# Top-32 attention and a leaky-ReLU MLP on one core: one reciprocal for two units, the even unit's split moved, weight pieces spread differently

## The chip, the cores and the metric

The kernel runs on one core of one Trainium2 chip. A core has a matrix engine (TensorE, "PE" in the profile; its weight loads are listed apart as "PEld"), a vector engine (VectorE, "DVE"), a scalar engine (ScalarE, "ACT"), a general engine (GpSimd, "POOL") and a queue engine (SyncE, "SP") that issues most of the DMAs. Each engine runs its own instructions in order and waits on semaphores for the others.

The metric is the device time of one execution in microseconds. Before the change it is 1431.69 us, the median of three runs (1431.59 to 1433.73). One further execution was profiled: 1433.87 us, of which the profile's span is 1431.8 us.

## What is computed

```python
# q, k, v: (8 batches, 8 heads, 576 tokens, 64)
scores = scale * q @ k.T                       # scale = 1/8
kth    = the 32nd largest score of each row
scores = where(scores >= kth, scores, -1e9)
attn   = exp(scores - rowmax)
attn   = attn / (attn.sum(-1) + 1e-9)
x      = attn @ v, heads side by side          # (4608 tokens, 512)
h      = x @ w_in                              # (4608, 2048)
out    = maximum(0.01 * h, h) @ w_out          # (4608, 512)
```

Everything is float32. The weights come in as 64-bit floating point numbers and are put together on the chip.

## The kernel before, in words

**Units.** Two heads of one batch make a pair of heads; 128 query rows of such a pair (both heads, so 2 x 576 scores per partition) make a *unit*. There are 144 units. Batch by batch, 16 units have whole blocks of 128 rows, and two gather the 64 rows left over of two pairs of heads each. `steps` is the list of the units, and the kernel goes through them two at a time: an *even* step s and an *odd* step s+1 make one turn of the main loop. The text calls units s and s+1 a pair of units.

**What happens to a unit.** PE computes the scores (L237), ACT copies them to `s_sb` (L246). DVE finds the 32 largest (`top_k`, L263): it folds the 576 scores into a maximum and a minimum half (two TENSOR_TENSOR on L270, one for each head), and then alternates MAX8 (L276) and MATCH_REPLACE8 (L281) four times. `limits` (L285) makes two small vectors, on ACT (`nleast`) and on POOL (`nbias`, L292 and L293). `mask` (L295) and `exponents` (L299) run on ACT and leave the row sums in `z`; `sums` (L303) adds 1e-9 on ACT and writes `ze`; `reciprocals` (L307) is one DVE instruction on a 128x2 tile; `normalize` (L311) multiplies, one ACT instruction for each head. `split` (L314) then takes the float32 weights apart into two 16-bit halves, two POOL copies of 128x1152 with a DMA to DRAM behind each, and `transpose` (L324) reads them back transposed by a DMA transpose into `wT` (three buffers). With `wT`, PE weighs the values (`weigh_whole`, L356, L365 in the profile), and the result is copied by ACT into `x` (L388).

**Order of the work.** The order is written out by hand, engine by engine, in `even` (L729) and `odd` (L781). In step s the unit itself (`cur`) is searched; the unit before it (`old`) gets its limits, mask and exponents; the one before that (`older`) is finished. So an even unit s has its exponents and `sums` in odd step s+1, and its reciprocal, normalization, split and transpose at the start of even step s+2. An odd unit s+1 has its exponents, `sums`, reciprocal and normalization within even step s+2, and its split and transpose in odd step s+3. Both are weighed at the end of even step s+4 (`values_at`, L637). The generator `picks` lets the DVE search be cut: in the even step the old unit's reciprocal stands after the third round, so one pair of MAX8 of this unit and then the odd unit's L270 follow.

**The MLP.** When all units of 128 tokens (the first four chunks, `EARLY`) or of 256 tokens are weighed, a chunk of the MLP becomes ready (`attended`). Its matmuls are fed to PE in slices: `mlp_steps(budget)` is called seven times in each step, and each call emits matmuls up to a budget. Evictions of a finished PSUM tile (ACT, L492 for `gT`, L526 for `o_sb`) are put off to the next `catch_up`. The large chunks use a seven-product scheme, whose sums of matrices (`gT`, `top`, `o_sb` on L443) run on POOL: `sum_now(2)` late in the even step, `sum_now(3)` in the odd step.

**The first four units.** `first_steps` (L839) handles units 0 to 3 and at the same time rounds the weights: 16 pieces (the first in two parts), each read by a DMA of 1 MB, copied on POOL (L129), worked on by ACT, PE and DVE (L135 to L158). `round_more` moves the queue of pieces on by one. Before the change it is called twice in each of units 0 and 1, three times in each of units 2 and 3, and the rest after them, where DVE has no search to do. `BESIDE` decides from which piece on the even ones use the `narrow` PSUM tile.

Of the kernel before, what the change touches and what calls it, by code (L numbers as in the profile page):

```python
# [20 lines left out]
def kernel(  # L21
# [13 lines left out]
    nc = tc.nc  # L35
# [64 lines left out]
    FIRST = 4  # L100
    BESIDE = 2 * FIRST + 3

# [182 lines left out]
    def limits(u):  # L285

        largest, least_kept = u.tops[:, :, 0, 0], u.tops[:, :, ROUNDS - 1, 7]
        u.nleast = small.tile([P, 2], F32, name="nleast")
        u.nbias = small.tile([P, 2], F32, name="nbias")
        u.z = small.tile([P, 2], F32, name="z")  # L290
        nc.scalar.activation(u.nleast, least_kept, AF.Copy, bias=0.0, scale=-1.0)  # L291
        nc.gpsimd.tensor_tensor(u.nbias, least_kept, largest, ALU.subtract)  # L292
        nc.gpsimd.tensor_scalar(u.nbias, u.nbias, SCALE, None, ALU.mult)  # L293
# [8 lines left out]

    def sums(u):  # L303
        u.ze = small.tile([P, 2], F32, name="ze")
        nc.scalar.activation(u.ze, u.z, AF.Copy, bias=1e-9, scale=1.0)

    def reciprocals(u):  # L307
        u.rz = small.tile([P, 2], F32, name="rz")
        nc.vector.reciprocal(u.rz, u.ze)  # L309

# [326 lines left out]
    def values_at(n):  # L637

        return (n | 1) + (2 if n in HASTY else 3)

    steps = units

    def unit(n):
# [3 lines left out]
    for n, u in enumerate(steps):  # L647
        ch, _ = x_at(u.b * S + u.q0)
        done_tokens[ch] += u.rows * len(u.pairs)
        if done_tokens[ch] == CHUNKS[ch] * HP:  # L650
            ready_at.append(((values_at(n) | 1) if n >= FIRST else FIRST - 1, ch))
    assert [ch for _, ch in ready_at] == list(range(len(CHUNKS)))
# [20 lines left out]
    with tc.manual_schedule():  # L673
# [41 lines left out]
        def values(s, spare):  # L715
            weighed = []
            for n in range(FIRST, len(steps), 2):
                if values_at(n) != s:
# [10 lines left out]
        def even(s):  # L729
# [5 lines left out]
            next(picks, None)  # L735
            if older:
                reciprocals(older)
            for _ in range(4):
# [7 lines left out]
            catch_up()  # L746
            if older:
                normalize(older, 0)
                normalize(older, 1)
                if not in_haste:  # L750
                    split(older)
                    transpose(older)
                else:
                    transpose_in_haste(older)
            mlp_steps(budget)
            if old:
                exponents(old, 0)
                exponents(old, 1)
                sums(old)
            if older and in_haste:  # L760
# [20 lines left out]
        def odd(s, new, ps, weighed):  # L781
# [12 lines left out]
            if older and not in_haste:  # L794
                split(older)
                transpose(older)
            keep(weighed)
            if new:
                keep_scores_of(new, ps)
            if older and in_haste:  # L800
                transpose_in_haste(older)
                if old:
                    exponents(old, 0)
                    exponents(old, 1)
                    sums(old)
                keep_transposed(older)
# [11 lines left out]
            if old and not in_haste:  # L818
                exponents(old, 1)
                sums(old)  # L820
            for _ in range(4):
# [17 lines left out]
        def first_steps():  # L839

            load_weights(0)
            load_qk(0)
            load_weights(1)
# [3 lines left out]
            load_qk(3)  # L847
            next(jobs[0], None)
            round_more()
            first = first_scores(steps[0])  # L850
            next(first, None)
            next(first, None)
            round_more()
            first = first_scores(steps[1])
            next(first, None)
            new = ps = None
            for s in range(FIRST):
# [6 lines left out]
                next(picks, None)  # L864
                if s < 2:
                    next(picks, None)
                if s == 0:
# [7 lines left out]
                if old:  # L875
                    exponents(old, 0)
                    exponents(old, 1)
                    sums(old)
                if s < 2:
                    next(picks, None)  # L880
                next(picks, None)
                next(picks, None)
                round_more()
                if old:
                    reciprocals(old)
                    normalize(old, 0)
                    normalize(old, 1)
                if s >= 2:
                    next(picks, None)
                    next(picks, None)  # L890
                    round_more()
                for _ in picks:
# [17 lines left out]
            exponents(b, 1)  # L910
            sums(b)
            round_more()
            reciprocals(b)
# [5 lines left out]
            round_more()  # L919
# [75 lines left out]
```

## Time and profile before

| | |
|---|---|
| median of three runs | 1431.69 us |
| profiled execution | 1433.87 us |
| its span | 1431.8 us |
| DVE busy | 1319.2 us (92%) |
| PE busy | 1347.2 us (94%) |
| ACT busy | 1023.0 us (71%) |
| POOL busy | 709.8 us (50%) |
| DVE MAX8, L276 | 636.3 us, 1152 instructions |
| DVE MATCH_REPLACE8, L281 | 460.6 us, 864 instructions |
| DVE TENSOR_TENSOR, L270 | 212.8 us, 288 instructions, mean 778 ns |
| DVE RECIPROCAL, L309 | 21.7 us, 144 instructions, mean 151 ns |
| POOL COPY, L321 (split) | 316.8 us, 284 instructions, mean 1144 ns |

How to read it: a line of the profile names the source line, the engine, the operation, what it writes and reads, and the shapes. "Busy" is the union of the spans of a group. In a timeline each line begins with the start in us and the time from the first start to the last end of the group; `x2` means two instructions put together, and a bracket gives the idle time of the engine before it and what ended it. A matmul's end is modelled, so that PE's busy share says less than it seems to. The chain of work that ended last is followed back from the last instruction, at each step to what released it.

### The profile page before, as it was taken

Reading aid. Unit: us, or ns where it says so; the run is one execution under the profiler, and the core shown is the slowest. Engines: PE = TensorE matmul, PEld = TensorE weight load, DVE = VectorE, ACT = ScalarE, POOL = GpSimd, SP = SyncE. Lnnn points to the kernel's source line nnn. Section 1 sums busy time; section 2 is a strip of 40 time slices with the busy share of each in tenths; the row PEclk is TensorE's granted clock in tenths of the full one; section 3 lists DMA queues with packets and bytes.
Section 4 is the critical chain, followed back from the end, with each engine's and each line's share of the span. In section 5 each row is a group of like instructions: output and inputs, shape, how many; then the busy total and the mean of one; then the engine's idle time right before and its main releaser. Section 6 shows DMA issues by size and latency. Waiting matters only on the chain.

```text
span 1431.8 us, 27705 instructions
## 1 busy us (share of the span) xinstructions
PE 1347.2 (94%) x9794; PEld 1031.4 (72%) x9794; DVE 1319.2 (92%) x3412; ACT 1023.0 (71%) x2144; POOL 709.8 (50%) x796
## 2 busy tenths in 40 slices
PE   6679599969999999999999999999999999999998
PEld 2234354447778888878888888888878888888887
DVE  7989999899999999999999999999999999999700
ACT  6866767677777777777777777777777777777621
POOL 2332373335555555555555555555555555555512
PEclk9889899989999999999999999999999999999999
DMA  7772545655666556756666556655676565655400
GB/s 291 250 222 67 140 134 172 193 141 133 165 185 174 144 144 186 196 152 139 177 175 173 141 164 174 186 142 155 175 182 168 141 157 142 169 145 136 125 12 15
DMA packets 399388, 224.91 MB, mean 157 GB/s; under 512 B 339216, under 2 KB 348432, under 8 KB 397328
## 3 DMA queue, kind: packets, MB, share of 16 engines
q1 hardware_dynamic: 398096, 222.08, 56.9%
q8 instruction: 77, 1.26, 0.4%
q10 hardware_dynamic: 1152, 1.05, 0.2%
q14 instruction: 63, 0.52, 0.1%
HBM read 46.14 MB, written 93.19 MB: 97 GB/s over the span
## 4 chain that ended last, share of the span: by engine, by line
DVE 70%; PE 18%; issue 6%; ACT 4%; DMA 1%; POOL 0%; DVEq 0%; POOLq 0%; ACTq 0%
DVE tops L276 34%; DVE pairs L281 26%; DVE pairs L270 7%; PE ph L504 4%; PE pz L518 4%; PE ph L405 3%; PE pz L596 2%; PE wide L365 2%; DMA raw<-in_weights_dram 1%; DVE rz L309 1%; PE wide L237 1%; ACT s_sb L300 1%; ACT s_sb L312 1%; DVE w_in L158 1%; PE narrow L237 0%
## 5 line engine op out<-in xcount | busy, mean ns | idle before, releaser
L276 DVE MAX8 tops<-pairs 128x8 f32<-128x288 f32 (+1 forms) x1152 | 636.3, 592 | 0.3 <-DVE rz L309 0.3
L504 PE MATMUL ph<-x,w_in 128*128 128x256 f32 x2048 | 457.5, 382 | 4.7 <-ACT gT L492 4.4
L281 DVE MATCH_REPLACE8 pairs<-tops,pairs 128x288 f32<-128x288 f32 (+1 forms) x864 | 460.6, 539 | 0.0
L504 PEld LDWEIGHTS ph<-x,w_in 128*128 128x128 f32 x2048 | 384.3, 190 | 84.0 <-issue 16.5
L321 POOL COPY split<-s_sb 128x1152 uint16<-128x1152 uint16 x284 | 316.8, 1144 | 186.1 <-ACT s_sb L312 186.1
L312 ACT ACTIVATE s_sb<-s_sb,rz 128x576 f32<-128x576 f32 x288 | 207.1, 766 | 151.6 <-DVE rz L309 151.5
L292 POOL TENSOR_TENSOR nbias<-tops 128x2 f32<-128x2 f32 x144 | 70.2, 488 | 401.5 <-DVE tops L276 398.0
L518 PE MATMUL pz<-w_out,gT 128*128 128x256 f32 x1024 | 226.5, 379 | 0.0
L270 DVE TENSOR_TENSOR pairs<-s_sb 128x576 f32<-128x576 f32 x288 | 212.8, 778 | 12.1 <-ACT s_sb L261 2.4
L300 ACT ACTIVATE s_sb<-s_sb,nbias 128x576 f32<-128x576 f32 x288 | 223.9, 785 | 0.0
L518 PEld LDWEIGHTS pz<-w_out,gT 128*128 128x128 f32 x1024 | 194.5, 190 | 26.6 <-issue 0.2
L297 ACT ACTIVATE s_sb<-s_sb,nleast 128x576 f32<-128x576 f32 x288 | 207.6, 768 | 4.7
L365 PE MATMUL wide<-wT,vt 128*64 128x128 f32 (+1 forms) x2560 | 156.4, 284 | 27.0 <-DMA wT<-apart 26.1
L365 PEld LDWEIGHTS wide<-wT,vt 128*64 128x64 f32 (+1 forms) x2560 | 128.3, 138 | 64.4 <-issue 34.0
L518 PE MATMUL pz<-raw,top 128*128 128x256 f32 x512 | 117.3, 384 | 4.6 <-ACT o_sb L526 4.4
L518 PEld LDWEIGHTS pz<-raw,top 128*128 128x128 f32 x512 | 95.2, 190 | 28.0 <-issue 8.0
L237 PE MATMUL wide<-kt,qt 64*64 64x352 f32 x1136 | 110.2, 458 | 0.0
L246 ACT COPY s_sb<-wide 128x704 f32<-128x704 f32 x142 | 108.0, 761 | 1.7 <-PE wide L237 1.7
L492 ACT ACTIVATE gT<-ph 128x512 f32<-128x512 f32 x128 | 75.3, 588 | 29.5 <-PE ph L504 29.5
L293 POOL TENSOR_SCALAR nbias<-nbias 128x2 f32<-128x2 f32 x144 | 84.7, 588 | 12.6
L291 ACT ACTIVATE nleast<-tops 128x2 f32<-128x2 f32 x144 | 28.6, 198 | 86.4 <-DVE tops L276 85.6
L526 ACT COPY o_sb<-pz 128x256 f32<-128x256 f32 x112 | 41.8, 374 | 60.8 <-PE pz L518 60.4
(70 smaller groups left out, 1238.4 us busy)
## 6 DMA issues: line engine op xcount, KB each, us to landing
apart<-split SPq DMA_DIRECT2D x284, 288.0 KB, 2.1
raw<-in_weights_dram SPq DMA_DIRECT2D x15, 1024.0 KB, 5.3
vt<-in_vk_dram SPq DMA_DIRECT2D x32, 320.0 KB, 3.8
qt<-in_qT_dram SPq DMA_DIRECT2D x32, 288.0 KB, 3.5
kt<-in_kT_dram SPq DMA_DIRECT2D x32, 288.0 KB, 3.6
out_dram<-o_sb SPq DMA_DIRECT2D x64, 128.0 KB, 2.2
wT<-apart SPq DMA_TRANSPOSE x142, 4.6
raw<-in_weights_dram SPq DMA_DIRECT2D x2, 512.0 KB, 4.3
```

What stands on the lines that cost most here:

```text
L237: nc.tensor.matmul(to[r0:r0 + LEFT, i, :], qt[d, q0:q0 + LEFT], kt[d, k0:k1], start=True, stop=True)
L246: nc.scalar.copy(u.both[:, :, k0:k1], to)
L270: nc.vector.tensor_tensor(pairs[:, :, n, :], u.both[:, :, 0:HS], u.both[:, :, HS:S], op)
L276: nc.vector.max(out=u.tops[:, i, r, :], in_=rest[i])
L281: nc.vector.match_replace(out=rest[i], in_to_replace=u.tops[:, i, r, :], in_values=rest[i], imm_value=LOWEST)
L297: nc.scalar.activation(u.s[i], u.s[i], AF.Prelu, bias=u.nleast[:, i:i + 1], scale=1.0, alpha=BELOW)
L300: nc.scalar.activation(u.s[i], u.s[i], AF.Exp, bias=u.nbias[:, i:i + 1], scale=SCALE, accum_out=u.z[:, i:i + 1])
L312: nc.scalar.activation(u.s[i], u.s[i], AF.Copy, bias=0.0, scale=u.rz[:, i:i + 1])
L321: nc.gpsimd.tensor_copy(split, pairs[:, :, h])
L365: nc.tensor.matmul(po[n * D:(n + 1) * D, side, 0:P], v_of[u.pairs[0]][k, at, side, :], u.wT[k, at + side * NKC if at + 1 < NKC else at, :] ...
L504: nc.tensor.matmul(ph[:, i, 0:n], w_in[c][:, f * P:(f + 1) * P], x[:, c, 0:n], start=(c == 0), stop=(c == HP - 1),)
L518: nc.tensor.matmul(to, g[:, f, :], w(f), start=(first and f == 0), stop=(f == HALF - 1), skip_group_check=not first)
```

## The change

There are three parts.

1. In `even`, a pair of units (s-2, s-1) gets one `ze` and one reciprocal on a 128x4 tile (`inverses_of_pair`) instead of two of each on 128x2. `z` becomes one tile for the pair. The shared reciprocal stands where the odd unit's stood, after the third round of the search in the even step. The last two units, which are finished in haste, and the first four keep their own.
2. The even unit's normalization and split, which stood at the start of the even step, now follow the shared reciprocal, after the even step's last MAX8 and one slice of MLP. Its transpose moves to the odd step, behind the odd unit's split and directly ahead of the odd unit's transpose.
3. In `first_steps` the first scores are computed before the first weight piece (a part of `qT` and `kT` is loaded first), each of the four units has three calls of `round_more`, and the values of units 0 to 3 are weighed at the end of even step 4, so that the first MLP chunk becomes ready in step 5 instead of step 3. `BESIDE` goes from 11 to 13.

```diff
-    BESIDE = 2 * FIRST + 3
+    BESIDE = 3 * FIRST + 1
...
-        u.z = small.tile([P, 2], F32, name="z")
+        if u.first is None:
+            u.of_pair = small.tile([P, 2, 2], F32, name="z")
+            u.z = u.of_pair[:, 0, :]
+        else:
+            u.z = u.first.of_pair[:, 1, :]
...
+    def inverses_of_pair(first, second):
+        ze = small.tile([P, 2, 2], F32, name="ze")
+        nc.scalar.activation(ze, first.of_pair, AF.Copy, bias=1e-9, scale=1.0)
+
+        def reciprocals():
+            rz = small.tile([P, 2, 2], F32, name="rz")
+            nc.vector.reciprocal(rz, ze)
+            first.rz, second.rz = rz[:, 0, :], rz[:, 1, :]
+
+        return reciprocals
...
-        return (n | 1) + (2 if n in HASTY else 3)
+        return (n | 1) + (2 if n in HASTY else 3) if n >= FIRST else FIRST
...
         def even(s):
...
-            if older:
-                reciprocals(older)
+            if in_haste:
+                older.invert()
...
-            if older:
+            if in_haste:
                 normalize(older, 0)
                 normalize(older, 1)
-                if not in_haste:
-                    split(older)
-                    transpose(older)
-                else:
-                    transpose_in_haste(older)
+                transpose_in_haste(older)
             mlp_steps(budget)
             if old:
                 exponents(old, 0)
                 exponents(old, 1)
-                sums(old)
+                invert = inverses(old) if in_haste else inverses_of_pair(older, old)
...
             if old:
-                reciprocals(old)
+                invert()
             for _ in picks:
                 pass
-            for _ in range(4):
+            mlp_steps(budget)
+            if older and not in_haste:
+                normalize(older, 0)
+                normalize(older, 1)
+                split(older)
+            for _ in range(3):
                 mlp_steps(budget)
...
         def odd(s, new, ps, weighed):
...
             if older and not in_haste:
                 split(older)
+                transpose(unit(s - 3))
                 transpose(older)
...
         def first_steps():
 
+            qk_of[0] = [loads.tile([P, S], F32, name=name) for name in ("qt", "kt")]
+            nc.sync.dma_start(qk_of[0][0][:, 0:P], qT[0][:, 0:P])
+            nc.sync.dma_start(qk_of[0][1], kT[0])
             load_weights(0)
-            load_qk(0)
+            nc.sync.dma_start(qk_of[0][0][:, P:S], qT[0][:, P:S])
...
-                if s >= 2:
-                    next(picks, None)
-                    next(picks, None)
-                    round_more()
+                next(picks, None)
+                next(picks, None)
+                round_more()
...
-            weighed = weigh(steps[0:2], ps_sc.tile([P, 2, 512], F32, name="wide", bufs=2))
-            round_more()
-            transpose(b)
             while begun[0] <= len(jobs):
                 round_more()
-            weighed += weigh(steps[2:4], ps_sc.tile([P, 2, 512], F32, name="wide", bufs=2))
-            keep(weighed)
-            attended(FIRST - 1)
+            transpose(b)
             load_more(FIRST - 1)
```

More of the change, by code (lines that the diff above doesn't have):

```diff
@@ L301, in exponents, with inverses, reciprocals @@
                              accum_out=u.z[:, i:i + 1])
-    def sums(u):
+    def inverses(u):
         u.ze = small.tile([P, 2], F32, name="ze")
         nc.scalar.activation(u.ze, u.z, AF.Copy, bias=1e-9, scale=1.0)
-    def reciprocals(u):
-        u.rz = small.tile([P, 2], F32, name="rz")
-        nc.vector.reciprocal(u.rz, u.ze)
+        def reciprocals():
+            u.rz = small.tile([P, 2], F32, name="rz")
+            nc.vector.reciprocal(u.rz, u.ze)
+        return reciprocals
+    def inverses_of_pair(first, second):
+        ze = small.tile([P, 2, 2], F32, name="ze")
+        nc.scalar.activation(ze, first.of_pair, AF.Copy, bias=1e-9, scale=1.0)
+        def reciprocals():
+            rz = small.tile([P, 2, 2], F32, name="rz")
+            nc.vector.reciprocal(rz, ze)
+            first.rz, second.rz = rz[:, 0, :], rz[:, 1, :]
+        return reciprocals
     def normalize(u, i):
@@ L637, in values_at @@
     def values_at(n):
-        return (n | 1) + (2 if n in HASTY else 3)
+        return (n | 1) + (2 if n in HASTY else 3) if n >= FIRST else FIRST
     steps = units
+    for n, u in enumerate(steps):
+        u.first = steps[n - 1] if n % 2 else None
     def unit(n):
@@ L650 @@
         if done_tokens[ch] == CHUNKS[ch] * HP:
-            ready_at.append(((values_at(n) | 1) if n >= FIRST else FIRST - 1, ch))
+            ready_at.append((values_at(n) | 1, ch))
     assert [ch for _, ch in ready_at] == list(range(len(CHUNKS)))
@@ L716, in values @@
             weighed = []
-            for n in range(FIRST, len(steps), 2):
+            for n in range(0, len(steps), 2):
                 if values_at(n) != s:
@@ L758, in even @@
                 exponents(old, 1)
-                sums(old)
-            if older and in_haste:
+                invert = inverses(old) if in_haste else inverses_of_pair(older, old)
+            if in_haste:
                 keep_transposed(older)
             if old:
-                reciprocals(old)
+                invert()
             for _ in picks:
                 pass
-            for _ in range(4):
+            mlp_steps(budget)
[4 more added lines that the diff above has]
+            for _ in range(3):
                 mlp_steps(budget)
@@ L804, in odd @@
                     exponents(old, 1)
-                    sums(old)
                 keep_transposed(older)
@@ L819, in odd @@
                 exponents(old, 1)
-                sums(old)
+            if s - 1 in HASTY:
+                old.invert = inverses(old)
             for _ in range(4):
@@ L847, in first_steps @@
             load_qk(3)
-            next(jobs[0], None)
-            round_more()
             first = first_scores(steps[0])
@@ L852, in first_steps @@
             next(first, None)
+            next(jobs[0], None)
             round_more()
@@ L864, in first_steps @@
                 next(picks, None)
-                if s < 2:
-                    next(picks, None)
                 if s == 0:
@@ L877, in first_steps @@
                     exponents(old, 1)
-                    sums(old)
-                if s < 2:
-                    next(picks, None)
+                    invert = inverses(old)
                 next(picks, None)
@@ L884, in first_steps @@
                 if old:
-                    reciprocals(old)
+                    invert()
                     normalize(old, 0)
                     normalize(old, 1)
-                if s >= 2:
-                    next(picks, None)
-                    next(picks, None)
-                    round_more()
+                next(picks, None)
+                next(picks, None)
+                round_more()
                 for _ in picks:
@@ L910, in first_steps @@
             exponents(b, 1)
-            sums(b)
+            invert = inverses(b)
             round_more()
-            reciprocals(b)
+            invert()
             normalize(b, 0)
@@ L917, in first_steps @@
             split(b)
-            weighed = weigh(steps[0:2], ps_sc.tile([P, 2, 512], F32, name="wide", bufs=2))
-            round_more()
-            transpose(b)
             while begun[0] <= len(jobs):
                 round_more()
-            weighed += weigh(steps[2:4], ps_sc.tile([P, 2, 512], F32, name="wide", bufs=2))
-            keep(weighed)
-            attended(FIRST - 1)
+            transpose(b)
             load_more(FIRST - 1)
```

## The prediction

> **What bounds the kernel now.** I read the page first: busy times, then the chain that ended last.
>
> ```profile
> span 1431.8 us, 27705 instructions
> PE 1347.2 (94%) x9794; PEld 1031.4 (72%) x9794; DVE 1319.2 (92%) x3412; ACT 1023.0 (71%) x2144; POOL 709.8 (50%) x796
> ...
> DVE 70%; PE 18%; issue 6%; ACT 4%; DMA 1%; POOL 0%; DVEq 0%; POOLq 0%; ACTq 0%
> ```
>
> VectorE (DVE) carries 70% of the chain. Windows of three pairs of units each show how near the rival is (columns: stretch, length, busy us of PE, PEld, DVE, ACT, POOL, then PE's granted clock, DMA share, GB/s); the first is an early pair.
>
> ```profile
> 150.52:168.16 17.64, 7.94 (x76) 5.42 (x76) 17.50 (x47) 11.87 (x26) 6.54 (x9) 0.71 0.62 153
> 679.60:732.52 52.92, 52.52 (x398) 43.23 (x397) 52.50 (x139) 40.41 (x88) 31.05 (x34) 1.00 0.67 176
> ```
>
> DVE is full from the first pairs on, PE only later. Up to about 1260 the chain is DVE's top-32 search almost without a break, one pair per 17.64 us; after 1265 it is PE, working off MLP matmuls until the end.
>
> Then one pair in order of time: DVE, ACT, POOL.
>
> ```profile
> 713.78 1.45 DVE L270 TENSOR_TENSOR pairs<-s_sb 128x576 f32<-128x576 f32 x2
> 715.15 0.15 DVE L309 RECIPROCAL rz<-ze 128x2 f32<-128x2 f32 x1
> 721.14 0.15 DVE L309 RECIPROCAL rz<-ze 128x2 f32<-128x2 f32 x1
> 722.64 1.43 DVE L270 TENSOR_TENSOR pairs<-s_sb 128x576 f32<-128x576 f32 x2
> ```
> ```profile
> 715.34 1.44 ACT L312 ACTIVATE s_sb<-s_sb,rz 128x576 f32<-128x576 f32 x2
> 721.32 1.44 ACT L312 ACTIVATE s_sb<-s_sb,rz 128x576 f32<-128x576 f32 x2 [2.53 <-DVE rz L309]
> ```
> ```profile
> 713.76 0.20 POOL L292 TENSOR_TENSOR nbias<-tops 128x2 f32<-128x2 f32 x1 [3.85 <-DVE tops L276]
> 716.84 2.23 POOL L321 COPY split<-s_sb 128x1152 uint16<-128x1152 uint16 x2 [2.21 <-ACT s_sb L312]
> 719.04 1.28 POOL L443 TENSOR_TENSOR top<-gT 128x512 f32<-128x512 f32 x1
> 720.40 1.28 POOL L443 TENSOR_TENSOR top<-top,gT 128x512 f32<-128x512 f32 x1
> 722.68 0.77 POOL L292 TENSOR_TENSOR nbias<-tops 128x2 f32<-128x2 f32 x1 [1.01 <-DVE tops L276]
> ```
>
> See that POOL has finished its long work (split, two sums) before L270 of the odd unit at 722.64. Last, the one late place where it hasn't:
>
> ```profile
> 1342.63 2.66 DVE L270 TENSOR_TENSOR pairs<-s_sb 128x576 f32<-128x576 f32 x2
> 1341.64 1.28 POOL L443 TENSOR_TENSOR top<-gT 128x512 f32<-128x512 f32 x1
> 1343.00 1.67 POOL L443 TENSOR_TENSOR top<-top,gT 128x512 f32<-128x512 f32 x1
> ```
>
> L270 took 2.66 instead of 1.43: its second half stood still while POOL did the second sum. MAX8 and MATCH_REPLACE8 beside a split keep their 0.44 and 0.74.
>
> **The change part by part.**
>
> *Reciprocals.* 144 become 75: units 4 to 141 (69 pairs) share one, which sits where the odd unit's was. In the pair above L270 to the first MAX8 takes 715.23-713.78 = 1.45 with the reciprocal between, 723.98-722.64 = 1.34 without; the next MAX8s are 0.02 shorter after it. 69 x 0.09 = -6.2 us, on the path. Bounds from what a reciprocal holds up in these rows, 0.07 to 0.15: -4.8 to -10.4.
>
> *The even unit's normalization and split.* They move from the start of the even step to behind that shared reciprocal. From 721.14 on, every gap is rigid: normalization 0.18 after the reciprocal, split 1.50 after that (715.34 to 716.84), so 1.68 after it; odd L270 1.50 after it (722.64-721.14). The split's first half will thus arrive 0.18 us into L270's first half, in each of 69 pairs. What happens then I take from the rows: nbias at 722.68, also just behind L270's start, needs 0.20 when alone (713.76) but ends 0.81 after L270's start, so it got in at 0.61. The split half (2.23/2, say 1.14) would run from 0.61 to 1.75. In the 1342.63 case L270 ended 0.62 after POOL (1345.29 and 1344.67). So L270 ends at 2.37 instead of 1.43: 69 x 0.94 = +64.9. Lower bound 0 (POOL waits until both halves are through; nothing in it can gain). Upper: an early pair of splits delayed two DVE operations, 1.33 and 1.36 instead of 0.42, 1.85 together: +128. I keep to 0.94, because the 1342.63 row is the same instruction with POOL waiting, 0.8 to 1.1 for the range.
>
> The Trainium skill (SBUF — State Buffer, "SBUF: two separate sides") says that the two engines share one port pair, locked for a whole instruction, the loser blocked, and that DVE operations with two SBUF inputs take part. By it the price would be the whole half split, 1.14 x 69 = 79, and the sum 14 higher; it also speaks against the place chosen.
>
> *What stands behind the split on POOL.* Two sums (pitch 1.35), the odd step's nbias, the other split, then the odd step's sums of gT. From the even L270 as 0: split halves 9.4-10.5 and 11.0-12.1, two sums to 14.8, nbias to 15.6, split to 17.8, then one sum (15 pairs), three (14) or none, 1.24 each. The next even L270 starts at 17.64-0.09+0.94 = 18.5. One sum ends at 19.0 and costs 0.4; of three, the second gets between the halves: 1.46. 14 x 1.86 = +26; bounds 0 (POOL 1 us earlier for one, none between) and 14 x 3.2 = +45 (two full collisions of 1.2 to 2).
>
> nbias later by 5 us: exponentials on ACT wait for it, but have until the shared reciprocal; ze was ready 2.5 us early (the wait at 721.32) and no longer has the 1.44 of normalization ahead. Cost 0; without this cover 1 us a pair.
>
> *SP and PE.* The even split's two DMAs issue later, and both transposes follow the odd split. They land about 7 us into the next even step; PE's weighing (718.74, 5.0 into it) then waits 2 us, and scores, loads and stores behind them slip likewise. The copies of scores end 4 us before DVE needs them, and PE gains 1 us of slack a pair from the slower DVE: cost 0; beyond 4 us, DVE would pay all of it. MLP evictions now stand behind the normalization on ACT: same cover.
>
> *First four units.* Scores first: the first L270 had waited 2.4 us. By kt's 3.6 us to landing, 2 us of matmul, 1.2 of copies and the first rounding behind them, I estimate it at 11.4 instead of 11.83. Two of six weight pieces move from the bare tail into the units; the tail's DVE waits are 1.46, 0.40 and 2.69, of which I take 3.0 as gone. Together -3.4; bounds +1 (copies delay rounding) and -7.0 (all). Chunk 0's MLP starts a step later: PE idles 9.7 of 17.64 in the first window above, which takes it. The fourth transpose must wait for weighing to free one of three wT buffers, holding SP; only a load of v is behind it, and scores needed 15 us later: 0, or 4.6 without cover.
>
> *Stalls.*
>
> ```profile
> DVE rz L309 <- ACT ze L305: 16.0, 7, 8.0
> ```
>
> Of these, 5.5 lie between 120 and 290, where ACT came late behind PE, and 2.3 at 1341. With the normalization out of the way and a slower DVE they go: -7.8 (bounds 0, -7.8). The old delay at 1342.63, 1.2, is counted in the 69 and comes off. What is late next is the port.
>
> *End.* From the last MAX8 (1352.5) to the end are 79 us. PE enters less behind; ACT's 4.6 us delay before the last limits, mostly behind PE, goes: -5 (0 to -6).
>
> **Sum:** -6.2+64.9+26-3.4-7.8-1.2-5 = +67.3. The profiled execution took 1433.87 (span 1431.8 and 2.1 around it), 2.2 over the median of the three runs; 1433.9+67.3 = 1501.2, less 2.2: **1499 us**.
>
> **The rivals.**
>
> (a) *No collision:* the split slips in only after L270 (it would have to come 0.43 later, or DVE keep the port for both halves). Then -6.2-3.4-5.5 remains, PE is fuller, and transposes 2 us later show at the end: about -13, 1419 us, faster. It decides where the split arrives past 0.61 after L270's start. For it: no row shows this split beside L270. Against: POOL and DVE took turns in the split rows (81.8 and 83.0, 90.6 and 91.6) and at 1342.63. 0.13.
>
> (b) *Splits collide, sums don't:* 1473. POOL's order has to run some us ahead of my addition. 0.20.
>
> (c) *Late transposes become the bound:* landing over 4 us beyond the old weighing, each further us costs 69; 1.3 us more gives about 1590. The order of queues allows it, the slack speaks against. 0.03.
>
> (d) *Gains and collisions cancel* (collision below 0.3 us): 1432. 0.03.
>
> My forecast's mechanism has 0.61; with (b) and (c), slower has 0.84, faster 0.13, within 0.2% (what a measurement of this kernel can tell from none) 0.03. Range: 0.8 a pair and no sums give 1433+55-6-7-9-5 = 1461, 1.1 and 45 give 1543; a little is added below: 1452 to 1542.
>
> **What would show it.** Odd L270 at about 2.4 instead of 1.43, split recorded as starting inside it and stretched; every fourth even L270 near 2.9; the period 18.5 to 20; 75 reciprocals; PE's share down. Odd L270 at 1.43 beside the split would prove me wrong at once; PE waits on wT with L270 waiting for scores would mean (c).

## The result, and the profile after

The changed kernel takes **1518.22 us** (median of four runs, 1515.71 to 1518.71) against 1432.71 us of the kernel before beside it (1431.59 to 1436.97), so 85.5 us slower; the ratio on record is 1.0588 with a 95% interval of 1.0562 to 1.0613 (the two medians alone give 1.0597). The prediction was 1499 us with a range of 1452 to 1542: the sign and the main mechanism held, the forecast was 19 us short.

The profiled execution took 1518.17 us with a span of 1516.4 us, 84.6 more than before. The page of the kernel after, its busy times, its chain and three of its groups (the numbers after the bar are busy time and mean ns of one, then idle time before):

```profile
span 1516.4 us, 27555 instructions
PE 1379.0 (91%) x9794; PEld 1047.4 (69%) x9794; DVE 1398.3 (92%) x3344; ACT 1014.2 (67%) x2075; POOL 725.7 (48%) x796
...
DVE 70%; PE 13%; issue 11%; ACT 4%; DMA 1%; POOL 0%; SPq 0%; DVEq 0%; POOLq 0%; ACTq 0%
...
L338 POOL COPY split<-s_sb 128x1152 uint16<-128x1152 uint16 x284 | 383.9, 1377 | 544.8 <-ACT s_sb L329 517.0
L270 DVE TENSOR_TENSOR pairs<-s_sb 128x576 f32<-128x576 f32 x288 | 297.5, 1073 | 12.2 <-ACT s_sb L246 2.9
```

Compare two numbers with the table of before: the L270 group went from 212.8 to 297.5 us for the same 288 instructions, which is 84.7 us, and the split's copies from 316.8 to 383.9. No semaphore says so. In the chain, the time shows as "issue" (6% before, 11% after), that is, as time in which the chain waits for nothing that the profile knows: behind the odd L270 of the pair shown below it is 1.48 us, behind that of the prediction's pair 0.53. PE's share of the chain fell from 18% to 13%.

Windows of the kernel after, an early pair and three later ones (columns as in the prediction):

```profile
157.24:175.78 18.54, 12.50 (x84) 7.53 (x84) 18.40 (x46) 14.31 (x32) 6.65 (x9) 0.72 0.55 145
718.26:773.85 55.59, 53.64 (x400) 43.71 (x399) 55.18 (x135) 39.79 (x83) 28.83 (x32) 1.00 0.62 162
```

Three pairs take 55.59 instead of 52.92 us, with DVE as full as before and PE with a little more room.

One pair of the kernel after in order of time, DVE, then ACT, then POOL:

```profile
564.87 1.45 DVE L270 TENSOR_TENSOR pairs<-s_sb 128x576 f32<-128x576 f32 x2
572.18 0.16 DVE L323 RECIPROCAL rz<-ze 128x4 f32<-128x4 f32 x1
573.68 2.37 DVE L270 TENSOR_TENSOR pairs<-s_sb 128x576 f32<-128x576 f32 x2
```
```profile
572.37 2.77 ACT L329 ACTIVATE s_sb<-s_sb,rz 128x576 f32<-128x576 f32 x4 [3.65 <-DVE rz L323]
```
```profile
573.88 3.18 POOL L338 COPY split<-s_sb 128x1152 uint16<-128x1152 uint16 x2 [8.14 <-ACT s_sb L329]
577.03 1.41 POOL L460 TENSOR_TENSOR o_sb<-o_sb 128x256 f32<-128x256 f32 x2
578.40 0.20 POOL L296 TENSOR_TENSOR nbias<-tops 128x2 f32<-128x2 f32 x1
578.84 2.23 POOL L338 COPY split<-s_sb 128x1152 uint16<-128x1152 uint16 x2
```

The even unit's split is recorded 0.20 us after the start of the odd unit's L270 (predicted 0.18) and takes 3.18 instead of the 2.23 that the odd unit's split takes 5 us later; L270 takes 2.37 instead of 1.43. All 69 odd L270s beside a split have this 2.37. And a place where the sums of `gT` meet the even unit's L270 (545.29, DVE, and 544.14 on, POOL):

```profile
545.29 2.50 DVE L270 TENSOR_TENSOR pairs<-s_sb 128x576 f32<-128x576 f32 x2
```
```profile
544.14 1.27 POOL L460 TENSOR_TENSOR gT<-gT 128x512 f32<-128x512 f32 x1
545.37 3.55 POOL L460 TENSOR_TENSOR gT<-gT,top 128x512 f32<-128x512 f32 x2
```

Of three sums the second and third together take 3.55 instead of 2.5 us, and L270 2.50 instead of 1.45.

### The profile page after: what moved, and what is told of

It is laid out like the page before. It is cut to its first block, busy times and chain, and to the rows that moved or that the text cites. A ratio compares the mean times of both kernels' runs of the same rounds, so it can differ in the third digit from the quotient of the medians.

```text
span 1516.4 us, 27555 instructions
## 1 busy us (share of the span) xinstructions
PE 1379.0 (91%) x9794; PEld 1047.4 (69%) x9794; DVE 1398.3 (92%) x3344; ACT 1014.2 (67%) x2075; POOL 725.7 (48%) x796
## 3 DMA queue, kind: packets, MB, share of 16 engines
q10 hardware_dynamic: 1152, 1.05, 0.2%
## 4 chain that ended last, share of the span: by engine, by line
DVE 70%; PE 13%; issue 11%; ACT 4%; DMA 1%; POOL 0%; SPq 0%; DVEq 0%; POOLq 0%; ACTq 0%
DVE tops L276 34%; DVE pairs L281 26%; DVE pairs L270 7%; PE ph L521 4%; PE pz L535 3%; PE wide L382 2%; PE ph L422 1%; ACT s_sb L329 1%; PE pz L613 1%; ACT s_sb L304 1%; PE wide L237 1%; DVE w_in L158 1%; DMA kt<-in_kT_dram 1%; ACT s_sb L301 0%; DVE rz L323 0%
## 5 line engine op out<-in xcount | busy, mean ns | idle before, releaser
L338 POOL COPY split<-s_sb 128x1152 uint16<-128x1152 uint16 x284 | 383.9, 1377 | 544.8 <-ACT s_sb L329 517.0
L521 PE MATMUL ph<-x,w_in 128*128 128x256 f32 x2048 | 462.3, 385 | 17.8 <-ACT gT L509 17.7
L270 DVE TENSOR_TENSOR pairs<-s_sb 128x576 f32<-128x576 f32 x288 | 297.5, 1073 | 12.2 <-ACT s_sb L246 2.9
L382 PE MATMUL wide<-wT,vt 128*64 128x128 f32 (+1 forms) x2560 | 165.6, 290 | 34.5 <-DMA wT<-apart 33.5
L382 PEld LDWEIGHTS wide<-wT,vt 128*64 128x64 f32 (+1 forms) x2560 | 135.6, 142 | 75.3 <-issue 40.5
L535 PE MATMUL pz<-raw,top 128*128 128x256 f32 x512 | 121.3, 393 | 11.2 <-ACT o_sb L543 10.7
L296 POOL TENSOR_TENSOR nbias<-tops 128x2 f32<-128x2 f32 x144 | 39.6, 275 | 110.7 <-DVE tops L276 110.7
L422 PE MATMUL ph<-w_in,x 128*128 128x512 f32 x128 | 63.9, 650 | 12.3 <-ACT scale L417 12.3
L405 ACT COPY x<-wide 128x256 f32<-128x256 f32 (+1 forms) x80 | 26.4, 340 | 71.4 <-PE wide L237 62.0
```

What stands on the lines that cost most here:

```text
L270: nc.vector.tensor_tensor(pairs[:, :, n, :], u.both[:, :, 0:HS], u.both[:, :, HS:S], op)
L338: nc.gpsimd.tensor_copy(split, pairs[:, :, h])
L382: nc.tensor.matmul(po[n * D:(n + 1) * D, side, 0:P], v_of[u.pairs[0]][k, at, side, :], u.wT[k, at + side * NKC if at + 1 < NKC else at, :] ...
L521: nc.tensor.matmul(ph[:, i, 0:n], w_in[c][:, f * P:(f + 1) * P], x[:, c, 0:n], start=(c == 0), stop=(c == HP - 1),)
L535: nc.tensor.matmul(to, g[:, f, :], w(f), start=(first and f == 0), stop=(f == HALF - 1), skip_group_check=not first)
```

## The experiments

**Theory:** a POOL instruction that is waiting when the first half of L270 ends gets in ahead of the second half, and DVE stands still until it is through; nothing else of the change costs much. (The two halves are the two instructions of L270. By the source one makes the maximum and one the minimum, each for both heads; they are not one for each head, as was said above.) The text calls this the port theory, after the prediction's word. The runs show that the two engines take turns, and what that costs; at which part of the chip they meet, no run shows. **Rivals:** the later transposes (and the weighing, scores and loads behind them on SP and PE), the new order on ScalarE with one reciprocal for four sums, and the new start. Eleven kernels were run; each was compared with the kernel before on the same chip.

The ledger, from each run's profiled execution. "Odd" and "even" are the sums of what the L270s of units from 5 on take beyond 1.43 us (odd) and 1.45 us (even); "begin" is the start of unit 4's L270; "waits" are those of DVE for `ze` and for copied scores between there and the last search; "tail" runs from the last MAX8 to the end.

| run | median us | ratio, 95% interval | span | odd | even | begin | waits | tail |
|---|---|---|---|---|---|---|---|---|
| before | 1432.71 | | 1431.8 | 3.4 | 2.0 | 103.2 | 8.0 | 79.3 |
| after | 1518.22 | 1.0588 [1.0562, 1.0613] | 1516.4 | 65.1 | 24.2 | 102.7 | 12.2 | 80.9 |
| e1_quarters | 1490.08 | 1.0390 [1.0369, 1.0411] | 1487.5 | 35.4 | 26.5 | 103.3 | 9.6 | 81.3 |
| e2_split_in_odd | 1474.49 | 1.0285 [1.0268, 1.0303] | 1471.5 | 6.2 | 28.1 | 103.1 | 20.7 | 81.8 |
| e3_old_start | 1520.06 | 1.0614 [1.0582, 1.0646] | 1518.4 | 65.2 | 22.4 | 104.1 | 14.7 | 80.9 |
| e4_sums_early | 1503.98 | 1.0478 [1.0444, 1.0512] | 1504.6 | 65.1 | 6.4 | 106.6 | 13.7 | 81.2 |
| v2_both | 1456.11 | 1.0163 [1.0142, 1.0184] | 1459.2 | -0.2 | 16.4 | 107.8 | 21.5 | 81.8 |
| e5_start_alone | 1433.62 | 1.0002 [0.9993, 1.0012] | 1431.3 | 3.5 | 2.1 | 104.0 | 6.3 | 79.6 |
| e6_late_transposes | 1433.53 | 1.0002 [0.9993, 1.0011] | 1431.2 | 3.5 | 2.1 | 103.3 | 7.1 | 79.3 |
| e7_collide_before | 1492.24 | 1.0408 [1.0392, 1.0424] | 1491.3 | 66.8 | 2.2 | 105.3 | 2.6 | 79.1 |
| e8_invert_earlier | 1513.10 | 1.0559 [1.0539, 1.0579] | 1507.9 | 81.6 | 2.1 | 103.8 | 11.7 | 77.2 |
| e9_invert_and_sums | 1435.14 | 1.0000 [0.9991, 1.0009] | 1435.8 | -0.2 | 2.2 | 107.6 | 14.7 | 79.1 |
| e10_old_start | 1436.94 | 1.0017 [1.0007, 1.0027] | 1437.4 | -0.2 | 2.1 | 105.5 | 18.6 | 79.0 |

Where the reciprocal is shared, a pair without any collision or wait takes 17.59 us instead of 17.65 (e2, e8, e9), so 69 x 0.06 = 4.1 us come off. With this, the columns' differences from before add up to each run's span within 0.7 us. For the kernel after: 61.7 + 22.2 - 0.5 + 4.2 + 1.6 - 4.1 = 85.1, measured 84.6. "Begin" differs by up to 5 us between kernels whose first steps are identical (see the last section), so the 0.5 says little.

### The collision alone, on the kernel before

```diff
             sum_now(2)
+            if old and s - 1 not in HASTY:
+                split(old)
...
             if older and not in_haste:
-                split(older)
                 transpose(older)
```

> The kernel before with one thing moved: the odd unit's split is issued at the end of the even step, right behind its own normalization, instead of in the odd step behind the limits. Everything else (144 reciprocals, the even unit's split at the start of the even step, transposes, start) is as in the kernel before. The normalization ends 1.5 us behind its start, so the copy's first half will arrive about 0.2 us into the odd unit's L270, just as the even unit's does in the kernel after. Port theory: every odd L270 takes 2.37 us instead of 1.43, 69 x 0.94 = 65 us, less the 3.4 us that odd L270s already lose: 1490 to 1500 us, and the even L270s stay at 1.45, since POOL is done earlier with everything behind. If the kernel after loses its time in anything else (the lateness of the even unit's work, ScalarE's order, the shared reciprocal), the odd unit's split done 2 us sooner costs nothing: 1430 to 1436 us. The odd unit's nbias waits behind the split by some 3 us; by the profile of before the work that needs it has that slack.

Measured: 1492.24 us, ratio 1.0408 (1.0392 to 1.0424). A pair of it, DVE and then POOL:

```profile
565.76 2.37 DVE L270 TENSOR_TENSOR pairs<-s_sb 128x576 f32<-128x576 f32 x2
```
```profile
566.01 3.14 POOL L321 COPY split<-s_sb 128x1152 uint16<-128x1152 uint16 x2 [2.01 <-ACT s_sb L312]
569.11 0.19 POOL L292 TENSOR_TENSOR nbias<-tops 128x2 f32<-128x2 f32 x1
```

It is the same 2.37 as in the kernel after, with the reciprocals, the transposes and the start of the kernel before. Doing a split *earlier*, with no instruction added, costs 59 us, since it arrives at the wrong moment. The odd column grows by 63.4; 5.4 of it comes back as shorter waits for `ze`. The nbias, 3 us later behind the split, costs nothing that shows.

### Half the copy between the halves

The even unit's split in four copies of 576 columns, at the same place.

```diff
-            nc.gpsimd.tensor_copy(split, pairs[:, :, h])
+            for c in range(0, 2 * S, S):
+                nc.gpsimd.tensor_copy(split[:, c:c + S], pairs[:, c:c + S, h])
```

> The kernel after, with the even unit's split written as four copies of 576 columns instead of two of 1152, at the same place. Nothing else moves. Port theory (POOL's copy gets in between the two halves of the odd unit's L270 and VectorE stands still until that one copy is through): only one copy of half the length stands between the halves, so each of the 69 odd L270s takes 1.43 + (0.95 - 0.57) = about 1.8 us instead of 2.37: 69 x 0.57 = 39 us less, about 1479 us. Rival 1 (the time comes from the later transposes, weighing and scores, or from ScalarE's new order; the stretched L270 is only where the waiting is recorded): the transposes are issued no earlier, so the time stays within 3 us of 1518. Rival 2 (the collision is proportional to the bytes that POOL moves, whatever the pieces): odd L270 stays near 2.37.

Measured: 1490.08 us, 28 less than the kernel after. Odd L270s take 1.94 to 1.95, not 1.8:

```profile
561.91 1.95 DVE L270 TENSOR_TENSOR pairs<-s_sb 128x576 f32<-128x576 f32 x2
```
```profile
561.45 0.67 POOL L347 COPY split<-s_sb 128x576 uint16<-128x576 uint16 x1 [7.48 <-ACT s_sb L329]
```

The first quarter needs the normalization of one head only, so it begins 0.46 us before L270; the second is the one that gets in between. Alone a quarter takes 0.67 (the line above) and costs L270 0.51; a half takes 1.14 and costs 0.94. The price follows the length of the one instruction that gets in, less 0.15 to 0.2 us. My 1.8 had taken a quarter for exactly half of a half. Both rivals of this run fall: the time did not stay within 3 us of 1518, and the same bytes cost about half of what they did.

### The even unit's split behind the odd L270

```diff
                 normalize(older, 1)
-                split(older)
...
             if older and not in_haste:
+                split(unit(s - 3))
                 split(older)
```

> The kernel after, with the even unit's split moved out of the even step into the odd one, after its limits and masks and directly before the odd unit's split; its normalization and the two transposes stay where the kernel after has them. Port theory: no copy waits beside the odd unit's L270, which goes back to 1.43 in all 69 pairs: about -62 us. POOL's work still reaches the next even L270 where three sums of gT or the sums of the weights are due, so some of the 22 us there stay: 1450 to 1465 us. Lateness theory (the rival: late transposes hold SyncE and TensorE): the transposes leave one split later than in the kernel after, so the time is the same or longer, 1518 to 1560, with odd L270 near 1.43 and VectorE waiting for scores instead.

Measured: 1474.49 us, 44 less than the kernel after, though the transposes are issued later still. DVE and POOL around one pair:

```profile
515.65 1.43 DVE L270 TENSOR_TENSOR pairs<-s_sb 128x576 f32<-128x576 f32 x2
...
524.43 3.14 DVE L270 TENSOR_TENSOR pairs<-s_sb 128x576 f32<-128x576 f32 x2
```
```profile
517.09 2.23 POOL L338 COPY split<-s_sb 128x1152 uint16<-128x1152 uint16 x2
520.50 2.24 POOL L338 COPY split<-s_sb 128x1152 uint16<-128x1152 uint16 x2 [1.18 <-DMA apart<-split]
522.70 1.28 POOL L460 TENSOR_TENSOR gT<-gT 128x512 f32<-128x512 f32 x1
523.93 3.02 POOL L460 TENSOR_TENSOR gT<-gT,top 128x512 f32<-128x512 f32 x2
```

The odd L270 is back at 1.43 in 58 of 70 units; the other 12 take 1.96 to 1.97, which is the 6.2 of the ledger. But POOL now has two splits in the odd step, the second waiting for a buffer that a DMA must empty, and the sums behind them reach the next even L270: 3.14 there in most of the places where the kernel after had 2.50. I had expected "some of the 22" to stay; 28 did, and the waits grew by 8.5. The rest of my estimate's miss is those waits; what makes them longer here was not separated.

### The sums alone, and both edits together

Sums early in the even step, behind limits and masks, as many as 7.2 us hold (in both kernels), with the split where the kernel after has it (first) or in the odd step (second):

```diff
+            sum_for(7.2)
             catch_up()
...
-            sum_now(2)
...
-            sum_now(3)
+            if s < 13:
+                sum_now(3)
```

> The kernel after with POOL's small sums in another place: all sums of gT and of the weights are done early in the even step, behind the masks' compares and ahead of the even unit's split, as many as about 7 us hold, and none behind the odd unit's split after step 13. The splits stay where the kernel after has them. Port theory: the even L270s lose their extra (22 to 24 us in all: 5.2 and 4.5 at units 14 and 16, about 1.05 at every eighth unit), the odd ones keep 2.37: 1495 to 1500 us. If the sums' extra was instead the price of the weighing's lateness, the even L270s go back to 1.45 and the time appears as waits elsewhere, 1513 to 1518.

Measured: 1503.98 us (1495.59 to 1506.38). The even column falls from 24.2 to 6.4, and odd stays at 65.1, as the port theory has it; of the 6.4, 4.0 are still at unit 14 and 1.7 at unit 42. The time is 4 us above the expected range. The profiled execution began its main loop at 106.6 instead of 102.7 us, which is as much; whether the other three did is not on record, and they lie as far as 11 us apart. The lowest is in the expected range.

> The last two edits together on the kernel after: even unit's split in the odd step, directly before the odd unit's, and POOL's small sums early in the even step. No copy and no sum is then left beside any L270. If the port was the whole loss, what remains is the shared reciprocal's gain, 69 x 0.06 = 4 us by the period of the split-in-odd run (17.59 against 17.65), so 1428 to 1431, a little under the kernel before. If the split-in-odd run's remaining 40 us over the kernel before are only in part collisions (28.1 us over 1.45 on the even L270s and 6.2 over 1.43 on the odd ones, against 2.0 and 3.4 before, so 29), the rest is lateness (transposes one split later, weighing and scores behind them, ScalarE's work behind TensorE's): 1474.5 - 29 = about 1445.

Measured: 1456.11 us. No odd collision is left, but even ones of over 0.2 us are, in 17 pairs. Here, before unit 66, the second split waited for its buffer and the sums behind it ran late (unit 66's L270, then POOL):

```profile
671.44 3.08 DVE L270 TENSOR_TENSOR pairs<-s_sb 128x576 f32<-128x576 f32 x2
```
```profile
669.77 1.15 POOL L338 COPY split<-s_sb 128x1152 uint16<-128x1152 uint16 x1 [1.13 <-DMA apart<-split]
670.88 3.02 POOL L460 TENSOR_TENSOR gT<-gT,top 128x512 f32<-128x512 f32 x2
```

So this run did not remove what it was meant to remove (16.4 us stayed), and it cannot say what the change would cost without collisions. The next two can.

### The shared reciprocal earlier

```diff
-            for _ in range(4):
+            for _ in range(4 if in_haste else 2):
                 next(picks, None)
```

> The kernel after with one number changed: in the even step the shared reciprocal stands two pieces of the search earlier on VectorE (in front of the third round's MAX8s instead of behind its MATCH_REPLACE8s, 2.8 us sooner, 4.6 us behind the even L270). The normalization and the split of the even unit follow it by the same 0.18 and 1.5 us, so the split runs from about 6.3 to 8.5 us and ends before the odd L270 at 8.8; the sums behind it end 2.8 us sooner too. Port theory: odd L270 back to 1.43 (-65 us), the even ones mostly back to 1.45 (-15 to -22 us): 1431 to 1440, with a little more of VectorE waiting for ze, which was there 3.2 to 5.8 us behind the even L270 in the kernel after. The place of the reciprocal and not the sharing is then what costs. If the later transposes and the order on ScalarE and SyncE carry the loss, 2.8 us win back only a part: 1480 or more.

Measured: 1513.10 us, only 5 less than the kernel after, and far from the 1431 to 1440 of the theory as I had applied it. DVE and POOL of one pair:

```profile
585.41 3.25 DVE L270 TENSOR_TENSOR pairs<-s_sb 128x576 f32<-128x576 f32 x2
```
```profile
582.83 2.23 POOL L338 COPY split<-s_sb 128x1152 uint16<-128x1152 uint16 x2 [5.37 <-ACT s_sb L329]
585.03 1.26 POOL L460 TENSOR_TENSOR top<-gT 128x512 f32<-128x512 f32 x1
586.37 1.67 POOL L460 TENSOR_TENSOR top<-top,gT 128x512 f32<-128x512 f32 x1
```

The split does end 0.35 us before the odd L270, at its full speed of 2.23. What I had not followed is what stands behind it on POOL: two sums of `gT` now lie exactly on the odd L270. The first holds up its first half, the second gets in ahead of its second half: 3.25 us in 29 pairs. In the other 28 pairs from unit 31 on, the two sums are shorter ones of `o_sb`, and L270 takes 2.17:

```profile
397.78 2.16 DVE L270 TENSOR_TENSOR pairs<-s_sb 128x576 f32<-128x576 f32 x2
```
```profile
397.40 1.92 POOL L460 TENSOR_TENSOR o_sb<-o_sb 128x256 f32<-128x256 f32 x2
```

The odd column is 81.6, worse than in the kernel after; up to unit 27, before those sums begin, every odd L270 but that of unit 15 is at 1.43. The even column is back at 2.1. The rival's number (1480 or more) is met, but not by its mechanism: waits and tail are no longer than in the kernel after.

So those two sums were moved as well, to where POOL is idle:

```diff
                 mask(old, 1)
+            sum_now(2)
             catch_up()
...
                 normalize(old, 1)
-            sum_now(2)
```

> The kernel with the earlier shared reciprocal, with POOL's two sums of the even step moved from behind the even unit's split to the start of the even step (behind the odd unit's nbias). In the run with the earlier reciprocal the split kept clear of the odd L270, but the two sums behind it ran from 8.4 to 11.4 us and hit it: 3.25 or 2.17 us in all pairs from unit 30 on (81.6 us over 1.43 in all). Port theory: with the sums gone from there nothing of POOL is beside any L270 but nbias, odd L270s return to 1.43 (-78 us against that run), and what is left is the shared reciprocal's gain of 4 us against some 4 us more of waits for ze: 1428 to 1438 us, that is, the kernel before again. If the loss follows from sharing the reciprocal, from the later transposes or from the order on ScalarE, it stays above 1460.

Measured: 1435.14 us against 1434.82, ratio 1.0000 (0.9991 to 1.0009). DVE and POOL:

```profile
567.20 1.43 DVE L270 TENSOR_TENSOR pairs<-s_sb 128x576 f32<-128x576 f32 x2
```
```profile
559.21 1.76 POOL L460 TENSOR_TENSOR top<-gT 128x512 f32<-128x512 f32 x1
561.05 1.28 POOL L460 TENSOR_TENSOR top<-top,gT 128x512 f32<-128x512 f32 x1
564.62 2.23 POOL L338 COPY split<-s_sb 128x1152 uint16<-128x1152 uint16 x2 [2.29 <-ACT s_sb L329]
```
```profile
L270 DVE TENSOR_TENSOR pairs<-s_sb 128x576 f32<-128x576 f32 x288 | 210.2, 770 | 9.7
```

This kernel has all three parts of the change: the shared reciprocal, the even unit's split behind it, both transposes in the odd step, the new start. Only two places in the order differ, and all 83 us are gone. With the first run above, in which the collision alone cost 59 us, that settles the question between the collision and its rivals.

### The lateness and the start, each alone

> The kernel before with one thing moved: the even unit's transposing DMA is issued in the odd step, directly before the odd unit's, as in the kernel after. Both splits, both normalizations, all reciprocals and the start stay as in the kernel before. This prices the lateness of the transposes by itself; nothing is added to the port. The prediction put it at 0 (cover: 4 us of slack of the scores ahead of VectorE, TensorE ahead of its work): 1433. If it carries what the split-in-odd run does not explain by collisions, 1440 to 1450, with the loss as waits of VectorE for the reciprocals' inputs or for scores in the pairs that have most MLP work beside them. Odd L270 at 1.43 in any case.

```diff
                     split(older)
-                    transpose(older)
...
                 split(older)
+                transpose(unit(s - 3))
                 transpose(older)
```

Measured: 1433.53 against 1433.51 us, ratio 1.0002 (0.9993 to 1.0011). Holding the even unit's transpose back to the odd step costs nothing, and the waits are those of before:

```profile
DVE rz L309 <- ACT ze L305: 15.1, 7, 8.0
```

> The kernel before with the third part of the change alone: the first four units' order, three weight pieces begun in each of them, their weighing moved to the step behind; reciprocals and splits stay as before. The prediction's term for it is -3.4 us (bounds -7.0 and +1): 1429. By the run that undoes the start in the kernel after (1520.1 against 1518.2) it is about -2, by the traces' begin of the main loop -0.5: 1431 to 1433. Rival: the first MLP chunk, which comes a step later, leaves TensorE behind and costs 3 to 8 us at 120 to 290 us: 1436 to 1441.

The edit is the change's third part on the kernel before, with nothing else; its core:

```diff
+            next(jobs[0], None)
             round_more()
             first = first_scores(steps[1])
             next(first, None)
+            round_more()
...
-                if s < 2:
-                    next(picks, None)
```

Measured: 1433.62 against 1433.51 us, ratio 1.0002 (0.9993 to 1.0012): neither the 3.4 us that I had counted on, nor the rival's loss.

> The kernel after with the third part of the change undone: the first four units, the weight pieces begun in them, and the weighing of those units are written as in the kernel before; the reciprocals and the split stay as in the kernel after. The prediction put the start at -3.4 us, so by it this takes 3.4 us longer (1521.6). By the traces of the two kernels the main loop began at 102.68 instead of 103.18 us, so only 0.5 is lost there (1518.7). Rival: the waits on the reciprocals' inputs between 120 and 290 us that were to go and did not (9.3 us, the pairs of units 18 to 22) come from the later begin of the first MLP chunk; then they shrink here and this is 5 to 9 us faster (1509 to 1513). Odd L270 stays at 2.37.

The converse, the third part undone in the kernel after; its core:

```diff
-        return (n | 1) + (2 if n in HASTY else 3) if n >= FIRST else FIRST
+        return (n | 1) + (2 if n in HASTY else 3)
...
+            weighed = weigh(steps[0:2], ps_sc.tile([P, 2, 512], F32, name="wide", bufs=2))
+            round_more()
             transpose(b)
```

Measured: 1520.06 us, 1.8 over the kernel after, with intervals that overlap (1.0582 to 1.0646 and 1.0562 to 1.0613), so that it can't tell 0.5 from 3.4 us. The waits did not shrink (14.7), so they don't come from the later first chunk.

### Can the shared reciprocal win?

The kernel of the earlier reciprocal and the early sums (the two diffs above), with the third part undone as in the last one:

> The kernel with the earlier shared reciprocal and the early sums, and with the third part of the change undone (the first four units as in the kernel before): the shared reciprocal without any collision and without the new start. In the profiled run with the new start the main loop began at 107.6 us, in those with the old start at 103.2 to 105.3. If the new start loses what these rows show, 1431 to 1433 us, some 0.1 to 0.3% under the kernel before; if the gain of the shared reciprocal (69 x 0.06 = 4 us) is eaten by the waits for ze (14.7 us against 8.0 without the one of the last units), 1434 to 1436, the same as before.

Measured: 1436.94 against 1434.31 us, ratio 1.0017 (1.0007 to 1.0027): a little slower than before, and 1 us over the upper of the two expected ranges. DVE's waits in this run (the second is that of the last units, in the tail):

```profile
DVE rz L323 <- ACT ze L319: 18.6, 12, 4.0
DVE rz L313 <- ACT ze L309: 7.8, 1, 7.8
```

The 4.1 us of the shared reciprocal are eaten by waits for `ze` (18.6 in the main loop against 8.0 before). No version here beats the kernel before.

## Why the prediction was right, and where it was off

The sum was +67.3 us for the profiled execution; 84.6 came in its span. Term by term:

- **Odd L270s, +64.9 less 1.2.** Measured 61.7 net, every one at the 2.37 us that the sum used. The step that carried it (nbias entering 0.61 us after L270's start, and the one late L270 of 2.66 us at 1342.63) was enough to price it: L270 ended 0.61 us after the copy that got in (575.44 and 576.05), 0.62 in the sum. The collisions that the kernel before already had were more than the one of 1.2 that came off: units 15 and 29 had them too (2.48 and 2.80 us), in all 3.4. The rule of the Trainium skill that I had set beside it (SBUF — State Buffer, "SBUF: two separate sides"), by which the shared port pair is locked for a whole instruction and the loser blocks, would by the estimate made there have given 79. The measurement says 0.94 for a copy of 1.14 us and 0.51 for one of 0.67: blocked for nearly, not quite, as long as the copy is recorded.
- **Sums at even L270s, +26.** Measured 22.2, differently spread, so that the near total is in part luck. One sum costs nothing (predicted 0.4): it is through 0.12 us after L270's start. Three sums cost 1.05 (predicted 1.46) at every eighth unit. But the weights' sums and those of `gT` at units 14 and 16 cost 3.7 (1.95 of it already before) and 3.1, and single even L270s at units 30, 58 and 142 lost 0.8, 1.9 and 1.2: places that I had not looked at.
- **Reciprocals, -6.2.** Measured -4.1: a pair is 0.06 shorter, not 0.09.
- **Transposes late, nbias late, 0.** Right for each alone (1.0002 in e6; and e7's nbias). In the whole change DVE waited 2.9 us for copied scores, which the prediction had at 0; they are in the next term but one.
- **Start, -3.4.** Measured -0.5 in the traces and nothing in the time. The first L270 came at 11.27 us (predicted 11.4), but took 2.31 instead of 1.43, beside a POOL copy of a weight piece that began at 11.42 and took 1.54. It is the main mechanism of this very prediction, which I had not applied there. And of the 3.0 us of tail waits "taken as gone", 2.75 were there again at other places (1.38 at 90.91, 1.37 at 100.68).
- **Waits for ze, -7.8.** This is the term that failed: "With the normalization out of the way and a slower DVE they go." They did not go; together with waits for copied scores they grew by 4.2:

```profile
DVE rz L323 <- ACT ze L319: 9.3, 8, 1.6
DVE pairs L270 <- ACT s_sb L246: 2.9, 4, 2.0
```

The prediction's reading of the chain is wrong here. "Up to about 1260 the chain is DVE's top-32 search" does not hold where 3.5 of these 8 us lie: from 180 to 280 us of the kernel before, 57% of the chain are PE's MLP matmuls of two lines alone (L596 and L405). Half of the reasoning holds where the reciprocals are separate: in e7, with a DVE slowed by the same collision, the waits fall from 8.0 to 2.6. But in all nine kernels that share the reciprocal they are 9.6 to 21.5, with or without collisions, against 2.6 to 8.0 in the four others (for `ze` alone 8.0 to 18.8, so that the lowest of the nine is level with the kernel before). Sharing goes with them; the late transposes (7.1) and the start (6.3) alone do not. Why ACT has `ze` later there was not separated by a run: what the trace shows is PE on the chain through that stretch (mostly L613 and L422, MLP matmuls, from 240 to 262 us), ACT's evictions behind it, and pairs of 20.1 us at units 20 and 22 in the kernel after as in e9, which has no collisions there (19.1 and 19.9 in the kernel before).
- **End, -5.** Measured +1.6. PE's remaining MLP work sets it, in every run between 77.2 and 81.8; a slower search did not let PE arrive with visibly less.

The three savings that were wrong (start, waits, end) make 2.9 + 12.0 + 6.6 = 21.5 us of the miss; the smaller gain of the reciprocals adds 2.1, and the collisions, 5.8 below my terms, take some back. For none of the three was there a row in which the saving could be seen; each was mainly a wait of before, taken as gone.

Of the rivals, (a) (no collision) needed the split 0.43 us later or elsewhere; e9 shows what it would have been worth: not 1419, but the kernel before again. (b) (splits only) was wrong on the sums, (c) (late transposes) cost nothing when tried alone (e6), (d) (cancelling) would have needed a collision of 0.3 us.

## What to carry to other kernels

Before moving an instruction of POOL, write down at which microsecond it and everything queued behind it will stand against the VectorE instructions that it can hold up, in every kind of period. Here these were the TENSOR_TENSOR on two SBUF tiles (1.43 to 2.37 us for the two) and, in the prediction's early rows, a 16-bit TENSOR_SCALAR (0.42 to 1.33), not MAX8 and MATCH_REPLACE8; e8 shows that curing the moved instruction alone can make its follower collide worse. Such a collision was found here in the duration of one VectorE group (here L270, 212.8 to 297.5 us) and in the "issue" share of the chain, not in any list of waits. And when one engine becomes slower, do not book the waits of others as gone without a row that shows them depending on it.

## What the runs showed of the hardware

- Two L270 instructions in immediate sequence do not keep POOL out: a copy or sum that waits gets in between them (the second half of L270 took 1.70 us beside the split, 0.75 undisturbed), and one that runs on into the first half holds that up (1.50 instead of 0.76 beside the first sum in e8). The MAX8 and MATCH_REPLACE8 beside the same copies keep their times (means of the 128x288 forms 442 and 437 ns in the kernel after, 442 and 439 before).
- The price is that of the one POOL instruction that gets in, not of all the work: four copies instead of two took 0.43 us of 0.94 off at the same bytes.
- POOL loses in these turns as well: the split's two copies take 3.18 instead of 2.23 us beside an L270, each of them recorded as started while the half of L270 that it has to wait for is still running (573.88, in a half that began at 573.68).
- The begin of the main loop lay between 102.7 and 107.8 us in the profiled executions, and over just this range in kernels whose first steps are identical (102.7 in the kernel after, 107.8 in v2_both). Differences of 4 us there say nothing about an edit.
